# Hashed attention with routed adapters: a new way from the inputs to score operands, and a reordered pipeline

## The chip, the cores and the metric

The kernel runs on one core of a Trainium2 chip. The core has five engines that run side by side and wait for each other by semaphores: TensorE (matrix products, here PE; its weight loads are listed as PEld), VectorE (DVE), ScalarE (ACT), GpSimd (POOL) and SyncE (SP), which here only issues transfers. SBUF is the working memory of 128 partitions, PSUM the memory that TensorE writes into, DRAM the chip's large memory. The metric is the device time of one execution in microseconds; the time of a kernel is the median of its runs.

## The reference

Two stages follow each other. The first is attention in which a query sees only the keys of its own hash bucket; the second adds to each token the output of two of eight small adapters.

```python
# q, k, v: (4, 8, 768, 64) float32; proj: (64, 6)
q_bits = (einsum('bhsd,dk->bhsk', q, proj) > 0)          # six sign bits per token
k_bits = (einsum('bhsd,dk->bhsk', k, proj) > 0)
mask   = bucket(q_bits)[..., :, None] == bucket(k_bits)[..., None, :]
scores = where(mask, q @ k.T / sqrt(64), -1e9)
attn   = exp(scores - max); attn /= sum(attn) + 1e-9
x      = (attn @ v)  ->  (3072, 512)                      # heads side by side
# adapters: w_gate (512, 8), A (8, 512, 16), B (8, 16, 512)
logits = x @ w_gate;  the two largest of the 8, softmax over the two -> w
out    = x + sum over the two e of  w_e * (x @ A[e]) @ B[e]
```

## The kernel before

Both versions treat two heads as a pair, 16 pairs in all, and never build the mask. The sign bits, as +0.5 and -0.5, are six further rows of the score operands `aug` beside the 64 features; a seventh row, 1.0 on the query side and -1.5 on the key side, completes it. Tokens of different buckets so get a score that the exponential turns to almost nothing. The exponentials are not normalised until after the product with the values: a column of ones in `vb` gives the sum, and a tiny uniform weight (`eps`, times the sum of all values) serves the queries that match no key.

A pair's inputs are loaded by SyncE, turned by TensorE in float32, copied out of PSUM by VectorE, hashed by TensorE, and the signs are put in place by eight small transfers:

```python
def load(self, p):                                   # q, k, v: all issued by nc.sync
    ...
    for i, src in enumerate((self.q, self.k)):
        nc.sync.dma_start(out=n[:, i], in_=src[b, h:h + 2]...)
def trans(self, p, g):                               # three times a pair
    ps = self.ps_t.tile([P, 512], F32, ...)
    for j in range(4):
        nc.tensor.transpose(out=ps[:, j*P:(j+1)*P], in_=self.nat[p][...], identity=self.ident)
    nc.vector.tensor_copy(out=self.qkT[p][:, g*512:(g+1)*512], in_=ps)
def hash(self, p):
    for j in range(4):
        nc.tensor.matmul(out=ps[32*j:32*j+32, :], lhsT=self.proj2,
                         rhs=self.qkT[p][:, j*384:(j+1)*384], start=True, stop=True)
    nc.vector.tensor_scalar(out=sgn, in0=ps, ..., op0=ALU.is_gt, op1=ALU.subtract)
    for j in range(4):
        for e in range(2):
            nc.sync.dma_start(out=av[:, :, e, :], in_=sgn[32*j+6*e:32*j+6*e+6, :]...)
def cast(self, p, e):                                # twice a pair, VectorE, 64 x 1536
    self.nc.vector.tensor_scalar(out=av[:, :, e, :], in0=self.qkT[p][64*e:64*e+64, :]...,
                                 scalar1=2.0 ** -5, ...)
```

The scores come in nine tiles of 128 x 1024 a pair, each with one exponential; then the values, the division, and the turn of the result for the adapters:

```python
def score(self, p, s):
    ps = self.ps_s.tile([P, 1024], F32, ...)         # two PSUM buffers
    while at < end:
        nc.tensor.matmul(out=ps[:, o:o+n], lhsT=aug[0:71, 2*h+1, kt*P:(kt+1)*P],
                         rhs=aug[0:71, 2*h, q0:q0+n], start=True, stop=True)
    nc.scalar.activation(out=self.P_[p][:, s*1024:end], in_=ps, func=ACT.Exp, scale=128.0)
def pvmm(self, p, h, i0, i1):
    for i in range(i0, i1):                          # query tiles
        for kt in range(T + 1):                      # six key tiles, then eps
            nc.tensor.matmul(out=pv[:, i, :], lhsT=..., rhs=vb[:, h, kt, :],
                             start=(kt == 0), stop=(kt == T))
def xtrans(self, p):                                 # ps_m: one PSUM buffer for all adapter work
    for i in range(self.T):
        nc.tensor.transpose(out=ps[:, i*P:(i+1)*P], in_=self.xb[b][...], identity=self.ident_bf)
    nc.vector.tensor_copy(out=self.xT[b][:, hp, :], in_=ps)
def moe_slot(self, p, s):
    # two pairs after a batch (4 pairs) is complete: lgz, route, lgz, route, zmtrans in one pair;
    # in the pair after that: six delta() steps, one a tile
    ...
def run(self):
    for p in range(N):
        for s in range(9):
            self.score(p, s)
            # the rest of the pair's work is put between the score tiles
            ...
    # after the last pair: norm, pvmm, norm, xtrans, xtrans, lgz, route, lgz, route, zmtrans, 6 x delta
```

Of the kernel before, what the change touches and what calls it, by code (L numbers as in the profile page):

```python
# [12 lines left out]
F32 = mybir.dt.float32  # L13
# [6 lines left out]
class Emitter:  # L20


    def __init__(self, ctx, tc, q, k, v, proj, w_gate, A, Bm, out):
# [11 lines left out]
        self.n_pairs = B * H // 2  # L35
# [6 lines left out]
        one = lambda n: ctx.enter_context(tc.tile_pool(name=n, bufs=1))  # L42
        self.singles = one("singles")
        self.natp = ctx.enter_context(tc.tile_pool(name="natp", bufs=3))
        self.qktp = ctx.enter_context(tc.tile_pool(name="qktp", bufs=2))
        self.sgp = ctx.enter_context(tc.tile_pool(name="sgp", bufs=2))
        self.pp = ctx.enter_context(tc.tile_pool(name="pp", bufs=2))
        self.xp = ctx.enter_context(tc.tile_pool(name="xp", bufs=2))
        self.smallp = ctx.enter_context(tc.tile_pool(name="smallp", bufs=4))
        ps = lambda n, b: ctx.enter_context(  # L50
            tc.tile_pool(name=n, bufs=b, space=bass.MemoryType.PSUM))
        self.ps_s = ps("ps_s", 2)
        self.ps_t = ps("ps_t", 2)
        self.ps_v = ps("ps_v", 1)
        self.ps_m = ps("ps_m", 1)


        sg = self.singles
        self.ident = sg.tile([P, P], F32, name="ident")
        make_identity(nc, self.ident)  # L60
        self.ident_bf = sg.tile([P, P], BF16, name="ident_bf")
        nc.vector.tensor_copy(out=self.ident_bf, in_=self.ident)

        self.proj2 = sg.tile([P, 32], F32, name="proj2")
        nc.vector.memset(self.proj2, 0.0)
        nc.sync.dma_start(out=self.proj2[0:64, 0:6], in_=proj)
        nc.sync.dma_start(out=self.proj2[64:128, 6:12], in_=proj)

        self.eps = sg.tile([P, P], BF16, name="eps")
        nc.vector.memset(self.eps, 2.0 ** -56)  # L70

        self.aug = []
        for i in range(2):
            a = sg.tile([P, 4, S], BF16, name=f"aug{i}")
            for h in range(2):
                nc.vector.memset(a[64:96, 2 * h, :], 1.0)
                nc.vector.memset(a[64:96, 2 * h + 1, :], -1.5)
            self.aug.append(a)

        self.vb = []  # L80
        for i in range(3):
            a = sg.tile([P, 2, T + 1, D + 1], BF16, name=f"vb{i}")
            nc.gpsimd.memset(a[:, :, 0:T, D:D + 1], 1.0)
            nc.gpsimd.memset(a[:, :, T:T + 1, D:D + 1], float(T))
            self.vb.append(a)
        nD = self.Dm // P
        self.nD = nD
        self.wa = sg.tile([P, nD, self.LZ], BF16, name="wa")
        self.Bcat = sg.tile([self.ER, self.Dm], BF16, name="Bcat")
        self.w_gate, self.A, self.Bm = w_gate, A, Bm  # L90

        self.nat, self.vn, self.qkT, self.sgn, self.P_, self.pv = {}, {}, {}, {}, {}, {}
        self.x, self.xb, self.xT, self.lz, self.tp = {}, {}, {}, {}, {}
        self.rt, self.zm, self.zmT, self.acc, self.sc = {}, {}, {}, {}, {}

    def load_moe(self):
        nc, P = self.nc, self.P
        nc.gpsimd.dma_start(out=self.wa[:, :, 0:self.E],
                            in_=self.w_gate.rearrange("(t p) e -> p t e", p=P))
        for t in range(self.nD):  # L100
            nc.gpsimd.dma_start(
                out=self.wa[:, t, self.E:].rearrange("p (e r) -> p e r", e=self.E),
                in_=self.A[:, t * P:(t + 1) * P, :].rearrange("e p r -> p e r"))
# [326 lines left out]
```

The softmax here doesn't subtract the row's maximum and nothing guards it: scores larger than these inputs give would overflow.

## Time and profile before

| | |
|---|---|
| time, median of 3 runs | 217.99 us (217.15 to 219.37) |
| span of the profiled execution | 216.4 us |
| exponentials of the scores | 144, 1024 ns each on average |
| float32 transposes of q and k | 192 on TensorE |
| copies of them out of PSUM | 48 on VectorE, 690 ns each |
| casts into the score operands | 32 on VectorE, 998 ns each |
| transfers of signs | 128, 4.5 KB each |

The profile is of one execution. Its page gives the busy time of each engine, then the span in 40 equal slices (a digit is the busy share in tenths; the row PEclk is the clock granted to TensorE), then groups of equal instructions with their count, mean duration and the idle time before them with what ended it. Names are those of the program, out<-in. In a list by time, the columns are start, duration, engine and line, operation, tiles and count; in a table of windows, the stretch and its length are followed by the busy time and count of PE, PEld, DVE, ACT and POOL, the clock, the share of the DMA engines and GB/s. A busy TensorE is not always one at its peak, since matmuls overlap and their ends are modelled.

### The profile page before, as it was taken

Reading aid. Unit: us, or ns where it says so; the run is one execution under the profiler, and the core shown is the slowest. Engines: PE = TensorE matmul, PEld = TensorE weight load, DVE = VectorE, ACT = ScalarE, POOL = GpSimd, SP = SyncE. Lnnn points to the kernel's source line nnn. Section 1 sums busy time; section 2 is a strip of 40 time slices with the busy share of each in tenths; the row PEclk is TensorE's granted clock in tenths of the full one; section 3 lists DMA queues with packets and bytes.
Section 4 is the critical chain, followed back from the end, with each engine's and each line's share of the span. In section 5 each row is a group of like instructions: output and inputs, shape, how many; then the busy total and the mean of one; then the engine's idle time right before and its main releaser. Section 6 shows DMA issues by size and latency. Waiting matters only on the chain.

```text
span 216.4 us, 5569 instructions
## 1 busy us (share of the span) xinstructions
PE 178.0 (82%) x2288; PEld 123.5 (57%) x2288; DVE 142.9 (66%) x303; ACT 144.1 (67%) x153; POOL 63.4 (29%) x98
## 2 busy tenths in 40 slices
PE   1647999999999997998979987989999879774341
PEld 0314286865868674756656866657678656463200
DVE  7771528675686768698756689796766875634541
ACT  2003679998999987677969976868999858730000
POOL 1694420623416050604133503305144110101000
PEclk9995569999999999999999999999999999997555
DMA  5895406062442616180746042533815000420024
GB/s 144 293 25 82 169 11 217 9 224 71 160 156 76 224 22 209 9 309 11 253 168 215 15 152 76 191 132 141 283 46 186 3 9 3 197 100 0 0 118 173
DMA packets 22874, 26.39 MB, mean 122 GB/s; under 512 B 8897, under 2 KB 21313, under 8 KB 22849
## 3 DMA queue, kind: packets, MB, share of 16 engines
q1 hardware_dynamic: 18016, 25.77, 35.2%
q0 software_dynamic: 4832, 0.27, 3.9%
q8 instruction: 18, 0.29, 0.6%
q14 instruction: 8, 0.06, 0.1%
HBM read 19.42 MB, written 6.29 MB: 119 GB/s over the span
## 4 chain that ended last, share of the span: by engine, by line
PE 52%; DVE 22%; DMA 9%; SPq 8%; issue 5%; ACT 2%; POOLq 0%; POOL 0%; DVEq 0%
PE s L190 20%; PE pv L209 12%; SPq L164 7%; PE tr L144 7%; PE hs L155 5%; DVE acc L303 5%; DMA nat<-in_k_dram 5%; PE dl L301 3%; DMA aug<-sgn 3%; DVE aug L172 3%; DVE sgn L158 2%; PE xtp L238 2%; DVE zm L276 2%; DMA nat<-in_q_dram 2%; DVE x L225 2%
## 5 line engine op out<-in xcount | busy, mean ns | idle before, releaser
L193 ACT ACTIVATE P<-s 128x1024 bf16<-128x1024 f32 x144 | 141.6, 1024 | 47.1 <-PE s L190 43.6
L190 PE MATMUL s<-aug 71*128 71x512 bf16 (+1 forms) x384 | 89.9, 336 | 5.0 <-DMA aug<-sgn 4.8
L209 PEld LDWEIGHTS <-P 128*128 128x128 bf16 x1152 | 51.3, 98 | 14.8 <-DVE x L225 1.0
L209 PE MATMUL pv<-vb,P 128*128 128x65 bf16 x1152 | 53.8, 194 | 0.9 <-DVE x L225 0.9
L190 PEld LDWEIGHTS <-aug 71*128 71x128 bf16 x384 | 32.5, 100 | 28.8 <-issue 13.0
L229 POOL CAST xb<-x 128x768 bf16<-128x768 f32 x16 | 13.2, 825 | 115.3 <-DVE x L225 115.3
L147 DVE COPY qkT<-tr 128x512 f32<-128x512 f32 x48 | 33.0, 690 | 14.1 <-PE tr L144 12.5
L144 PE MATMUL tr<-ident,nat 128*128 128x128 f32 x192 | 32.9, 296 | 8.1 <-DMA nat<-in_q_dram 3.9
L209 PE MATMUL pv<-vb,eps 128*128 128x65 bf16 x192 | 37.4, 195 | 0.0
L144 PEld LDWEIGHTS tr<-ident,nat 128*128 128x128 f32 x192 | 25.2, 152 | 14.4 <-issue 5.6
L172 DVE TENSOR_SCALAR aug<-qkT 64x1536 bf16<-64x1536 f32 x32 | 31.9, 998 | 0.9
L223 DVE RECIPROCAL ri<-pv 128x6 f32<-128x6 f32 x32 | 6.2, 193 | 29.5 <-PE pv L209 29.4
L303 DVE SCALAR_TENSOR_TENSOR acc<-dl,rt,x 128x512 f32<-128x512 f32 x24 | 17.9, 745 | 6.0 <-PE dl L301 6.0
L209 PEld LDWEIGHTS <-eps 128*128 128x128 bf16 x192 | 18.9, 98 | 0.0
L225 DVE TENSOR_TENSOR x<-pv,ri 128x384 f32<-128x384 f32 x32 | 17.8, 557 | 1.2
L126 POOL CAST vb<-vn 128x768 bf16<-128x768 f32 x16 | 13.3, 833 | 13.7 <-DMA vn<-in_v_dram 13.7
L128 POOL TENSOR_TENSOR vs<-vn 128x384 f32<-128x384 f32 x16 | 16.7, 1044 | 0.0
L301 PE MATMUL dl<-Bcat,zmT 128*128 128x512 bf16 x24 | 10.3, 431 | 7.7 <-DVE acc L303 6.8
L155 PE MATMUL hs<-qkT,proj 128*32 128x384 f32 x128 | 15.8, 542 | 0.0
L158 DVE TENSOR_SCALAR sgn<-hs 128x384 bf16<-128x384 f32 x16 | 8.9, 558 | 8.6 <-PE hs L155 7.0
L250 PE MATMUL lz<-wa,xT 128*128 128x136 bf16 x96 | 7.7, 235 | 4.3 <-DVE zm L276 3.6
L238 PE MATMUL xtp<-ident_bf,xb 128*128 128x128 bf16 x96 | 8.0, 219 | 3.0 <-POOL xb L229 1.4
(35 smaller groups left out, 79.6 us busy)
## 6 DMA issues: line engine op xcount, KB each, us to landing
nat<-in_q_dram SPq DMA_DIRECT2D x16, 384.0 KB
nat<-in_k_dram SPq DMA_DIRECT2D x16, 384.0 KB
vn<-in_v_dram SPq DMA_DIRECT2D x16, 384.0 KB
out_dram<-acc SPq DMA_DIRECT2D x12, 512.0 KB
aug<-sgn SPq DMA_DIRECT2D x128, 4.5 KB
wa<-in_moe_A_dram POOLq DMA_DIRECT2D x4, 32.0 KB, 3.1
Bcat<-in_moe_B_dram POOLq DMA_DIRECT2D x1, 128.0 KB, 3.5
proj<-in_proj_dram SPq DMA_DIRECT2D x2, 1.5 KB
```

What stands on the lines that cost most here:

```text
L128: nc.gpsimd.tensor_add(out=s3, in0=vn[:, :, 0:3, :], in1=vn[:, :, 3:6, :])
L144: nc.tensor.transpose(out=ps[:, j * P:(j + 1) * P], in_=self.nat[p][:, idx % 2, idx // 2, u * P:(u + 1) * P], identity=self.ident)
L147: nc.vector.tensor_copy(out=self.qkT[p][:, g * 512:(g + 1) * 512], in_=ps)
L155: nc.tensor.matmul(out=ps[32 * j:32 * j + 32, :], lhsT=self.proj2, rhs=self.qkT[p][:, j * 384:(j + 1) * 384], start=True, stop=True)
L164: nc.sync.dma_start(out=av[:, :, e, :], in_=sgn[32 * j + 6 * e:32 * j + 6 * e + 6, :].rearrange("p (u c) -> p u c", c=self.P))
L172: self.nc.vector.tensor_scalar(out=av[:, :, e, :], in0=self.qkT[p][64 * e:64 * e + 64, :].rearrange("p (j c) -> p j c", c=self.P), scalar1 ...
L190: nc.tensor.matmul(out=ps[:, o:o + n], lhsT=aug[0:71, 2 * h + 1, kt * P:(kt + 1) * P], rhs=aug[0:71, 2 * h, q0:q0 + n], start=True, stop=True)
L193: nc.scalar.activation(out=self.P_[p][:, s * 1024:end], in_=ps, func=ACT.Exp, scale=128.0)
L209: nc.tensor.matmul(out=pv[:, i, :], lhsT=lhsT, rhs=vb[:, h, kt, :], start=(kt == 0), stop=(kt == T))
L225: nc.vector.tensor_tensor(out=self.x[b][:, :, c:c + D], in0=pv[:, :, 0:D], in1=ri.unsqueeze(2).to_broadcast([P, T, D]), op=ALU.mult)
L301: nc.tensor.matmul(out=ps, lhsT=self.zmT[b][:, i * P:(i + 1) * P], rhs=self.Bcat, start=True, stop=True)
L303: nc.vector.scalar_tensor_tensor(out=self.acc[b][:, i, :], in0=ps, scalar=self.rt[b][:, i:i + 1], in1=self.x[b][:, i, :], op0=ALU.mult, op ...
```

## The change

The changed kernel computes the same. It takes another path from the inputs to the score operands, and lays the work out anew:

- **Hash.** VectorE turns q and k in 32x32 blocks; the hash multiplies these blocks with the projections laid out in `hst`, in two halves (`hf`) that add up in PSUM. The signs then stand in another order, so they are written to DRAM and read back in the order that `aug` wants.
- **Score operands.** GpSimd casts q and k to bf16 (`natcast`), TensorE turns them as bf16 with both heads in one transpose (`tbf`), VectorE copies them to `aug`.
- **Loads** of q, k and v are issued by GpSimd, so that SyncE has only the signs and the turns to issue.
- **Values.** One key block at a time for all six query tiles (`pvk`), so a block can start as soon as its exponentials are there; the uniform part is one wide matmul per head (`uni`).
- **Turn of the result** by the DMA crossbar (`dma_start_transpose`) except for the last pairs.
- **Adapters** are spread over four pairs. PSUM: `ps_v` has two buffers, `ps_m` and `ps_n` one each.
- **Start and end.** Dummy matmuls run at the start; pair 0 keeps the old float32 path, with half-loads on two queues. The last pair works in blocks of 256 queries (`lasts`, `norm3`, `turn3`), so its adapters can start before its last exponential.

The diff, cut to its core (`...` marks cuts):

```diff
-    def trans(self, p, g):
...
+    def turn32(self, p, i, h=None):
...
+        self.nc.vector.transpose(out=self.R[p][:, i, hs, :], in_=self.nat[p][:, i, hs, :])
+
+    def hash(self, p, hf):
...
         for j in range(4):
...
-            nc.tensor.matmul(out=ps[32 * j:32 * j + 32, :], lhsT=self.proj2,
-                             rhs=self.qkT[p][:, j * 384:(j + 1) * 384], start=True, stop=True)
+            rhs = self.R[p][:, j % 2, j // 2, :].rearrange("p (t f c) -> p f t c", f=2, c=32)[:, hf]
+            nc.tensor.matmul(out=self.hs[p][32 * j:32 * j + 32],
+                             lhsT=self.hst[:, hf].rearrange("p b i -> p (b i)"), rhs=rhs,
+                             start=(hf == 0), stop=(hf == 1), skip_group_check=True)
+
+    def sign(self, p):
...
+        nc.vector.tensor_scalar(out=sg, in0=self.hs[p], scalar1=0.0, scalar2=0.5,
                                 op0=ALU.is_gt, op1=ALU.subtract)
+        s2 = self.sgp.tile([P, T, 32], BF16, tag="s2", name=f"s2{p}")
+        nc.vector.tensor_scalar(out=s2, in0=sg, scalar1=self.ssc, scalar2=None, op0=ALU.mult)
+        d = self.dr[p] = self.scr.tile([T, P, 32], BF16, tag="dr", name=f"dr{p}")
+        nc.sync.dma_start(out=d.rearrange("t p c -> p t c"), in_=s2)
+
+    def signs(self, p):
...
+        src = self.dr[p].rearrange("t (j b i) c -> b j t (i c)", j=4, b=8)[0:7]
         for j in range(4):
...
+            nc.sync.dma_start(out=aug[64:71, j // 2, j % 2].rearrange("b (t c) -> b t c", t=T),
+                              in_=src[:, j])
+
+    def natcast(self, p, i):
...
+        self.nc.gpsimd.tensor_copy(out=self.nb[p][:, i].rearrange("p t h d -> p h t d"),
+                                   in_=self.nat[p][:, i].rearrange("p h (t d) -> p h t d", t=T))
+
+    def tbf(self, p, i, t):
...
+        self.nc.tensor.transpose(out=self.tr[p, i][:, t, :],
+                                 in_=self.nb[p][:, i, t].rearrange("p h d -> p (h d)"),
+                                 identity=self.ident_bf)
+
+    def augcopy(self, p, i):
...
+        nc.vector.tensor_copy(out=aug[:, 0, i, :], in_=self.tr[p, i].rearrange("p t c -> p (t c)"))
+        nc.vector.tensor_copy(out=aug[0:64, 1, i, :], in_=aug[64:128, 0, i, :])
...
+    def uni(self, p, h):
...
+        self.nc.tensor.matmul(out=pv, lhsT=self.eps,
+                              rhs=self.vb[p % 3][:, h, T:T + 1, :].to_broadcast([self.P, T, D + 1]),
+                              start=True, stop=False, skip_group_check=True)
+
+    def pvk(self, p, h, *kts):
...
+        for kt in kts:
+            for i in range(T):
...
+                self.nc.tensor.matmul(out=pv[:, i, :], lhsT=self.P_[p][:, o:o + P],
+                                      rhs=vb[:, h, kt, :], start=False, ...)
...
+    def turn(self, p):
...
+        self.nc.sync.dma_start_transpose(out=self.xT[b][:, hp, :, :],
+                                         in_=self.xb[p].rearrange("p t f -> p (t f)"))
...
+    def start(self):
+        self.loadqk(0, 0, 0, nc_s)
+        self.loadqk(0, 1, 0, nc_a)
...
+        for i in range(12):
+            nc.tensor.matmul(out=w, lhsT=self.wz[:, 0:128], rhs=self.wz, start=True, stop=True)
...
+    def slot(self, p, s):                     # one score tile s of pair p; nx = p + 1, n2 = p + 2
+        TS = {1: [(0, t) for t in range(6)],
+              2: [(1, t) for t in range(4)], 3: [(1, 4), (1, 5)]}
...
+        self.score(p, s, [lambda a=a: self.tbf(nx, *a) for a in TS.get(s, ())])
+        if s == 0 and p:
+            self.hash(nx, 1)
+            self.sign(nx)
+        if s == 8:
+            self.hash(n2, 0)
...
+            if s == ((1, 3), (5, 7))[p == 0][i]:
+                self.augcopy(nx, i)
+        if s in (2, 4, 5, 6):
+            r = (2, 4, 5, 6).index(s)
+            self.turn32(n2, r // 2, r % 2)
+        self.moe1(p, s)
...
+        if s == (4 if p else 8):
+            self.signs(nx)
+        if s == 6 and not last:
+            self.turn(p - 1)
+        if s in ((0, 1) if p else (4, 5)):
+            self.loadqk(p + 3, s % 4, None, self.nc.gpsimd)
+        if s == 2 and p:
+            self.loadv(p + 2, self.nc.gpsimd)
...
+        if s in (5, 6):
+            self.natcast(n2, s - 5)
+        if s == 0 and p:
+            self.vcast(nx)
...
+    def moe1(self, p, s):                     # spread over the four pairs after a batch
...
+        LS = {2: ((0, 0), (0, 1)), 3: ((0, 2),), 4: ((0, 3), (1, 0), (1, 1)),
+              6: ((1, 2), (1, 3), (2, 0)), 7: ((2, 1), (2, 2), (2, 3))}
...
+            Z = {2: {5: G0}, 3: {5: G1}}.get(hp, {})
+            L = {1: G0, 2: G1}.get(hp)
+            D = {3: {4: (0, n), 6: (1, n), 7: (2, m)},
+                 0: {4: (3, n), 6: (4, n), 7: (5, m)}}.get(hp, {})
...
+    def lasts(self, s):                       # the last pair, in blocks of 256 queries
...
+        if s >= 2:
+            self.pv3((s - 2) // 3, (s - 2) % 3)
+        if s == 4:
+            self.norm3(0, "pool")
+        if s == 5:
+            self.turn_pe(self.N - 2)
+            self.turn3(0)
...
+    def end(self):                            # what is left after the last exponential
...
+        self.norm3(2, "act")
+        self.delta(b, 0, S)
+        self.turn3(2)
+        ... routing of the last tiles, then
+        self.delta(b, 5, S)
+        self.store(b, 2, 1, self.nc.scalar)
```

## The prediction

> **What bounds the kernel now.** I read the page of the profile first, then the start times of the exponentials on ScalarE, then windows cut at the pair boundaries that those starts give, and last the instructions of one quiet pair in order of time. The kernel is a pipeline over 16 head pairs. A pair has nine score tiles and each tile ends in one exponential, 144 in all, so the exponentials are the program's clock. The page:
>
> ```profile
> span 216.4 us, 5569 instructions
> PE 178.0 (82%) x2288; PEld 123.5 (57%) x2288; DVE 142.9 (66%) x303; ACT 144.1 (67%) x153; POOL 63.4 (29%) x98
> ...
> ACT  2003679998999987677969976868999858730000
> PEclk9995569999999999999999999999999999997555
> ```
>
> No engine is full over the span, but the ACT row is thin in the first four slices (5.4 us each) and empty in the last four, and dips in the middle. The exponentials in order of time (start, duration, count, idle time before):
>
> ```profile
> 18.83 1.02 ACT L193 ACTIVATE P<-s 128x1024 bf16<-128x1024 f32 x1 [16.81 <-PE s L190]
> ...
> 40.95 3.77 ACT L193 ACTIVATE P<-s 128x1024 bf16<-128x1024 f32 x4 [0.15 <-PE s L190]
> ...
> 189.62 2.14 ACT L193 ACTIVATE P<-s 128x1024 bf16<-128x1024 f32 x2 [0.67 <-PE s L190]
> ```
>
> The first starts at 18.83 us, the last ends at 191.76: a head of 18.8 and a tail of 24.7 us hold no exponential. Four in 3.77 us, the last taking 1.02, give (3.77-1.02)/3 = 0.92 us from start to start when nothing holds ScalarE up: 9 x 0.92 = 8.3 us per pair, 132 us for all. Windows of pair 4 (no expert work), 6 (routing), 7 (the six expert outputs of a batch) and the tail (stretch, its length, then busy time per engine):
>
> ```profile
> 60.00:69.30 9.30, 9.30 (x137) 6.84 (x136) 6.54 (x12) 8.67 (x9) 3.52 (x6) 1.00 0.40 133
> 78.70:91.70 13.00, 11.31 (x167) 8.59 (x165) 9.92 (x35) 9.31 (x11) 3.83 (x6) 1.00 0.31 97
> 91.70:104.00 12.30, 11.21 (x142) 7.52 (x140) 10.22 (x18) 9.22 (x9) 3.47 (x5) 1.00 0.42 143
> 191.70:216.40 24.70, 9.13 (x90) 5.13 (x90) 10.77 (x34) 0.50 (x3) 0.83 (x1) 0.62 0.16 64
> ```
>
> In the quiet pair TensorE is busy for the whole 9.30 us: it is the bound. In pairs 6 and 7 no engine is full; VectorE comes to 10 us and TensorE and VectorE wait on each other through a single PSUM buffer. The tail is a serial chain at a granted clock of 0.62. TensorE's costs, from starts in the quiet pair (a busy time is stretched by the pipeline, so I take start to start):
>
> ```profile
> 60.65 0.60 PE L144 MATMUL tr<-ident,nat 128*128 128x128 f32 x4
> ...
> 61.11 0.59 PE L190 MATMUL s<-aug 71*128 71x256 bf16 x3
> ...
> 62.55 0.85 PE L155 MATMUL hs<-qkT,proj 128*32 128x384 f32 x8
> ...
> 63.34 0.61 PE L190 MATMUL s<-aug 71*128 71x512 bf16 x2
> ```
>
> Four fp32 transposes take 61.11-60.65 = 0.46 us (115 ns each), the hash 63.34-62.55 = 0.79. From the following starts in the same view, a score tile takes 0.44, fourteen value matmuls 0.45 (32 ns each), six bf16 transposes 0.34 (57 ns each). Sum of a pair: scores 9 x 0.44 = 3.96, values 84 x 0.032 = 2.69, fp32 transposes 12 x 0.115 = 1.38, hash 0.79, transposes of the output 0.34: 9.16, against 9.27 measured from first exponential to first exponential.
>
> **What the skill says.** The Trainium skill, "TensorE: Matmul & The Clock Gate", What's actually happening: the array starts at half clock and is released after some 3.4 us of sustained work. The slices' clock row agrees in kind (5 and 6 around 16 to 32 us, 5 again at the end). "VectorE: DVE Perf Modes", The three transpose paths: VectorE turns only 32x32 blocks; the DMA crossbar needs 1309 ns for 128x128 bf16. No run of this kernel has either. "DMA: Bandwidth & Descriptors", Two DMAs through the same engine are not ordered: a read of what another DMA wrote must wait for its completion; the new path through DRAM pays two landings. "SBUF — State Buffer", SBUF: two separate sides: VectorE in its two-port modes and GpSimd exclude each other for a whole instruction. The trace doesn't show that as a loss: GpSimd's casts of 128x768 take 825 and 833 ns on average beside a busy VectorE.
>
> **The change part by part, for one pair in the middle.** TensorE: fp32 transposes become 12 bf16 ones, 12 x 0.057 = 0.68 (saves 0.70). The 12 eps matmuls become two of 390 columns, 2 x 390 x 0.44/1024 = 0.33, and 72 value matmuls remain, 2.30: 2.63 for 2.69. The output's six transposes go to the crossbar: saves 0.34. The hash keeps its 768 moving columns per column group, in two halves: about 0.88. Sum 3.96+2.63+0.68+0.88 = 8.15, now under ScalarE's 8.3. Expert work per batch is 24 routing matmuls of 136 columns (0.06 each, 1.44), six transposes (0.34), six outputs of 512 columns (6 x 0.22 = 1.3): 3.1 us. Before, it fell on two pairs; now on four, 0.77 each. So TensorE needs 8.9 in pairs 4 to 15.
>
> VectorE, with a fixed part of about 0.16 us and 0.96 elements per ns (384 fp32 elements took 557 ns, 512 took 690): it loses three copies of 0.69 and two casts of 1.0 and the 0.55 copy of the turned output. It gains four 32x32 turns of 384 elements (0.55 each, an estimate from those rows: 2.2), two sign steps (0.36+0.2), two PSUM copies (0.55 each, the rate of the like copy before) and two bf16 copies of 64 partitions (0.35 each, estimate). With two normalisations (2 x 0.75) that is 6.1 us. Routing of three row tiles (about 1.9), the zT copies (0.36), three outputs (3 x 0.745) add 1.9 to 2.6: 8.0 to 8.7 us.
>
> GpSimd: vb and its sums 0.83+1.04+0.46+0.46, two new casts 1.65, xb 0.83, three load issues at 0.9 (weight loads it issues took 0.91 to 1.03): 8.0 us, with stores up to 9.8 in some pairs. ScalarE: 8.3 plus at most one 0.22 exponential.
>
> So four engines need 8.0 to 8.9 us and the largest is TensorE. Before, pairs 6 and 7 took 1.1 to 1.7 us more than TensorE's busy time; the change moves each wait a slot or more away from its producer and doubles some PSUM buffers, so I choose a loss of 0.6: 9.5 us for pairs 4 to 15. Pairs 2 and 3, without expert work, 8.6; pair 1, with values left over from pair 0, 9.0.
>
> Head: twelve dummy matmuls raise the clock by about 6 us; half-loads issued from two queues land near 4, as the first one did (3.95). Then six transposes (0.7), copy (0.55), hash (0.7), a second hash (0.7), and VectorE's four sign steps (0.56 each) one after another: first score about 9.7, first exponential about 10.6. Pair 0: nine exponentials at 0.92, plus a wait of some 3 us at its end, since the signs of pair 1 are issued in its last slot: two issues (0.72 each) and a landing of 1.8 (the issue at 15.37 released TensorE at 17.17). I take 11.5.
>
> Tail: the last pair works in column blocks of 256 so that its routing starts early. After the last exponential, VectorE has two normalisation steps (0.6), six outputs (4.5), two routings of two tiles (2 x 1.4) and copies (0.9): 8.8, some 1.2 of waits, and the last store. Before, the last output ended at 212.76 and the program at 216.4, 3.6. I take 13.5.
>
> Sum: 10.6 + 11.5 + 9.0 + 2 x 8.6 + 12 x 9.5 + 13.5 = 175.8. The measured time was 1.6 above the span (217.99 against 216.4), so 177.4 us. Of the 40.6 us gained, the head and pair 0 give 10.0, the middle 19.4 (27.98+131.7 before, 26.2+114 after), the tail 11.2.
>
> **Rivals.** (1) The signs set the pace. Signs of pair p+1 need: the score tile and second hash half of pair p (0.9), VectorE (about 0.8), a DRAM write of 768 pieces of 64 bytes (1.8 as above plus about 1.3: the software queue's 4832 small packets took 3.9% of 16 engines' 216 us, 28 ns each), two issues and a landing (0.75+1.8): 7.4 us inside a pair of 9.5. It holds unless VectorE is late or the write issue is slow; at 10.5 a pair the total is 189. For it: before, signs already made score tiles wait (PE s <- DMA aug<-sgn 4.8 us). (2) VectorE is the bound. If a 32x32 turn of fp32 ran at half rate, 1.6 us more: 10.2 a pair and 186. Against: the casts it replaces cost more. (3) GpSimd is late: its casts now feed TensorE, and at 8 to 9.8 us of work a lock by VectorE or slower issues would show; 10 a pair, 183. (4) Everything overlaps and ScalarE bounds at 8.6: 166. (5) The steady pairs gain nothing and only head and tail do: about 197.
>
> **Range and chances.** The middle is 12 pairs, so 0.5 us of error per pair is 6 us; rivals 1 to 3 give 183 to 189, rival 4 gives 166. I take 168 to 191. For slower, a pair would have to take 13 us on average, as only the two expert pairs do now: faster 0.95, same 0.03, slower 0.02.
>
> **What would show it.** After the change: first exponential near 10.6; pairs 4 to 15 near 9.5 between first exponentials, all alike instead of 9.2 and 13; TensorE's busy share about 90%, ScalarE's near 80%, VectorE's and GpSimd's near 75%; tail near 13.5. If score matmuls wait for the signs' DMA, rival 1 is right; if transposes wait for GpSimd's casts, rival 3; a mean of 32x32 turns near 0.95 us would be rival 2. A pair over 10.9 would prove the middle wrong altogether.

## The result, and the profile after

The changed kernel takes 191.8 us (median of four runs, 188.62 to 195.41); the kernel before took 218.45 us on the same chip (217.15 to 219.37). The ratio is 0.8661 [0.8596, 0.8726]; here and below, ratios leave disturbed runs out. 177.4 us had been predicted, with a range of 168 to 191, so the median lies just above the range and the gain is 26.7 us instead of 40.6. The profiled execution took 189.62 us; all stages below are read from it.

The page of the changed kernel: span, busy time of each engine, then two of the rows in 40 slices (4.7 us each).

```profile
span 187.6 us, 5480 instructions
...
PE 166.5 (89%) x2200; PEld 107.3 (57%) x2200; DVE 137.8 (73%) x366; ACT 146.0 (78%) x161; POOL 122.4 (65%) x189
...
ACT  3459547996999899999997969889998989785100
PEclk9999958999999999999999999999999999999555
```

The shares are close to those predicted (TensorE 90%, ScalarE 80%, VectorE and GpSimd 75%), except GpSimd's. ScalarE's row is dense from the eighth slice to the thirty-sixth; before, the dense part ended with dips and four slices behind it were empty. But there is a 5 in the clock row at the sixth slice, where the row of ScalarE is thin too. The exponentials by time (start, duration, count, and in brackets the idle time before them with what ended it):

```profile
10.60 1.02 ACT L301 ACTIVATE P<-s 128x1024 bf16<-128x1024 f32 x1 [0.85 <-PE s L294]
...
24.26 1.02 ACT L301 ACTIVATE P<-s 128x1024 bf16<-128x1024 f32 x1 [2.75 <-PE s L294]
26.46 1.02 ACT L301 ACTIVATE P<-s 128x1024 bf16<-128x1024 f32 x1 [1.18 <-PE s L294]
...
46.14 17.19 ACT L301 ACTIVATE P<-s 128x1024 bf16<-128x1024 f32 x18 [1.49 <-PE s L294]
...
112.43 7.99 ACT L301 ACTIVATE P<-s 128x1024 bf16<-128x1024 f32 x8 [1.41 <-PE s L294]
```

The first one starts at 10.60, as predicted. Pair 1 starts at 24.26 after a wait of 2.75 us, pair 3 at 46.14 after 1.49, pair 10 at 112.43 after 1.41: the waits sit where a new pair begins. Where they are short, 18 exponentials run on over two pairs in 17.19 us. The same stages as windows, the stretch and its length, then busy times, clock, DMA share and GB/s (head, pair 0, pair 1, pairs 4 to 15, tail):

```profile
0.00:10.60 10.60, 8.82 (x37) 3.75 (x39) 7.11 (x18) 3.79 (x7) 3.58 (x24) 1.00 0.81 263
10.60:24.26 13.66, 10.68 (x97) 4.70 (x100) 9.29 (x17) 8.87 (x10) 13.00 (x16) 0.95 0.38 120
24.26:36.12 11.86, 11.86 (x149) 7.89 (x153) 6.70 (x16) 8.68 (x10) 9.66 (x15) 0.76 0.45 127
...
54.79:171.50 116.71, 110.48 (x1629) 76.25 (x1621) 93.64 (x255) 106.71 (x115) 77.47 (x111) 1.00 0.63 166
171.50:187.60 16.10, 7.18 (x47) 3.37 (x46) 9.14 (x34) 0.84 (x3) 0.40 (x1) 0.55 0.24 98
```

The first clock record of this profile is at 5.96 us; ahead of it the clock row and the 1.00 of the head are no measurement. The dummy matmuls start 0.43 us apart there; in the profile with the loads put first (below), whose clock rises at 4.15 us, they start 0.43 apart before and 0.22 after. In the kernel before the first record is at 13.3 us, so the 9s at the start of its clock row say nothing either.

Set beside the kernel before (cut at its own pair starts) and the prediction, in us:

| stage | before | predicted | after | after minus predicted |
|---|---|---|---|---|
| head, to the first exponential | 18.83 | 10.6 | 10.60 | 0.0 |
| pair 0 | 13.23 | 11.5 | 13.66 | 2.2 |
| pairs 1 to 3 | 27.98 | 26.2 | 30.53 | 4.3 |
| pairs 4 to 15 | 131.72 | 114.0 | 116.71 | 2.7 |
| tail | 24.64 | 13.5 | 16.10 | 2.6 |
| span | 216.4 | 175.8 | 187.6 | 11.8 |

Of the 28.8 us gained in the span, the head gives 8.2, the middle 15.0 and the tail 8.5; pairs 0 to 3 lose 3.0. The chain that ended last, by line, says what stands in the middle now, with a transfer in second place:

```profile
PE s L294 20%; DMA aug<-dr 17%; PE pv L325 9%; PE hs L179 4%; DMA dr<-s 4%; PE tr L221 4%; PE warm L534 3%; PE lz L429 3%; DVE R L169 2%; DVE acc L503 2%; DMA nat<-in_k_dram 2%; DVE aug L230 2%; DVE zm L467 2%; PE dl L499 1%; DVE aug L267 1%
```

L294 are the score matmuls, `aug<-dr` the reads of the signs, `dr<-s` their write. One turn of that loop, from the chain in order of time (start, duration, what), at the end of pair 2:

```profile
35.58 0.44 PE s L294 x3
...
36.54 0.37 DVE sg L188
...
36.94 0.37 DVE s L191
...
37.32 2.71 DMA dr<-s
...
40.50 4.89 DMA aug<-dr
45.39 0.05 issue
45.44 0.61 PE s L294 x3
```

Of VectorE's two steps the first takes what was predicted (0.37 against 0.36), the second 0.37 against 0.2; the write takes 2.71 against 3.1. The read takes 4.89 against 1.8. The score matmuls of pair 3 wait for it until 45.39.

### The profile page after: what moved, and what is told of

Its sections match the earlier page's. It is cut to its first block, busy times and chain, and to the rows that moved or that the text cites. A ratio compares the mean times of both kernels' runs of the same rounds, so it can differ in the third digit from the quotient of the medians.

```text
span 187.6 us, 5480 instructions
## 1 busy us (share of the span) xinstructions
PE 166.5 (89%) x2200; PEld 107.3 (57%) x2200; DVE 137.8 (73%) x366; ACT 146.0 (78%) x161; POOL 122.4 (65%) x189
## 4 chain that ended last, share of the span: by engine, by line
PE 48%; DMA 22%; DVE 17%; issue 6%; POOL 3%; SPq 1%; ACT 0%; DVEq 0%; POOLq 0%
PE s L294 20%; DMA aug<-dr 17%; PE pv L325 9%; PE hs L179 4%; DMA dr<-s 4%; PE tr L221 4%; PE warm L534 3%; PE lz L429 3%; DVE R L169 2%; DVE acc L503 2%; DMA nat<-in_k_dram 2%; DVE aug L230 2%; DVE zm L467 2%; PE dl L499 1%; DVE aug L267 1%
## 5 line engine op out<-in xcount | busy, mean ns | idle before, releaser
L294 PE MATMUL s<-aug 71*128 71x256 bf16 (+1 forms) x396 | 93.0, 326 | 7.8 <-DMA aug<-dr 7.1
L294 PEld LDWEIGHTS <-aug 71*128 71x128 bf16 x396 | 35.1, 98 | 28.9 <-issue 9.6
L361 POOL CAST xb<-x 128x768 bf16<-128x768 f32 x15 | 12.4, 824 | 30.5 <-DVE x L345 26.0
L169 DVE STREAM_TRANSPOSE R<-nat 128x384 f32<-128x384 f32 (+1 forms) x58 | 31.8, 573 | 0.5
L221 PE MATMUL tr<-ident_bf,nb 128*128 128x128 bf16 x180 | 27.0, 224 | 0.2 <-DVE sg L188 0.2
L211 POOL CAST nb<-nat 128x768 bf16<-128x768 f32 x30 | 24.0, 827 | 0.1
L221 PEld LDWEIGHTS <-nb 128*128 128x128 bf16 x180 | 16.5, 101 | 4.9 <-issue 1.4
L230 DVE COPY aug<-tr 128x768 bf16<-128x768 bf16 x30 | 16.3, 543 | 3.6 <-PE tr L221 2.3
L179 PE MATMUL hs<-R,hst 128*32 128x192 f32 x240 | 16.3, 344 | 0.0
L155 POOL CAST vb<-vn 128x768 bf16<-128x768 f32 x16 | 13.3, 830 | 4.4 <-DMA vn<-in_v_dram 3.0
L231 DVE COPY aug<-aug 64x768 bf16<-64x768 bf16 x30 | 13.0, 433 | 1.2
L499 PE MATMUL dl<-Bcat,zT 128*128 128x512 bf16 x24 | 10.1, 437 | 0.7 <-DVE acc L503 0.6
L313 PE MATMUL pv<-vb,eps 128*128 128x390 bf16 x30 | 10.1, 336 | 0.2 <-POOL vb L160 0.2
```

What stands on the lines that cost most here:

```text
L169: self.nc.vector.transpose(out=self.R[p][:, i, hs, :], in_=self.nat[p][:, i, hs, :])
L179: nc.tensor.matmul(out=self.hs[p][32 * j:32 * j + 32], lhsT=self.hst[:, hf].rearrange("p b i -> p (b i)"), rhs=rhs, start=(hf == 0), stop= ...
L211: self.nc.gpsimd.tensor_copy(out=self.nb[p][:, i].rearrange("p t h d -> p h t d"), in_=self.nat[p][:, i].rearrange("p h (t d) -> p h t d", ...
L221: self.nc.tensor.transpose(out=self.tr[p, i][:, t, :], in_=self.nb[p][:, i, t].rearrange("p h d -> p (h d)"), identity=self.ident_bf)
L230: nc.vector.tensor_copy(out=aug[:, 0, i, :], in_=self.tr[p, i].rearrange("p t c -> p (t c)"))
L294: nc.tensor.matmul(out=ps[:, o:o + w], lhsT=aug[0:71, h, 1, kt * P:(kt + 1) * P], rhs=rhs, start=True, stop=True)
```

## The experiments

Four theories for the missing 11.8 us were put to the test. **Signs:** the reads of the signs land late because they share the DMA engines with the loads, turns and stores. **Lock:** VectorE stands still while GpSimd works. **Clock:** TensorE's clock falls to half after a wait, above all in pair 1. **Tail order:** in the last pair, the division of the second block stands behind the routing of the first. Their rivals were that the turns by the crossbar are the disturbance, that DMA traffic plays no part, and that TensorE's own work sets the pace whatever the transfers do. In the expectations these are T1 (T1a: the loads are to blame; T1b: the path through DRAM itself), T2 (T2b for the second copy), T4 and T3; T5 is the worth of the dummy matmuls at the start.

Landing times below are from the completion records of the sign transfers, issue to last completion. Pairs are counted from 0, and a pair's length is from its first exponential to that of the next pair, for the last pair to the end of its last exponential. Stage lengths are those of one profiled execution each.

### Leave out the sign reads

The four reads of signs in each pair are left out. The rows of `aug` that they fill keep a constant for one head of the pair, and for the other what the copy from PSUM put there, so the mask of this kernel is not that of the reference; everything else runs on.

```diff
 def signs(self, p):
         for j in range(4):
-            nc.sync.dma_start(out=aug[64:71, j // 2, j % 2]..., in_=src[:, j])
+            pass
```

> Leaves out the four reads of the signs per pair (pairs 1 to 15 get no hash rows; the write to DRAM stays). Theory T1 (the last gap of each pair, 1.2 to 3.8 us before the next first exponential, is the wait for the signs): the gaps shrink to about 1.2, pairs 4 to 15 fall from 9.73 to about 9.2 on average, pairs 0 to 2 lose 5 us together, time about 177 against 189 for the changed kernel. Rival R1 (the gaps are TensorE and VectorE work and only labelled by the DMA): under 2 us change.

Measured: 184.03 us (183.42 to 184.58), ratio 0.8497 [0.8415, 0.8580]. Pairs 0 to 3 take 39.3 us instead of 44.2, so 4.9 of the 6.5 us that they lost against the prediction hung on the reads, with the fall of the clock in pair 1, which does not occur here. Pairs 4 to 15 take 9.63 us on average instead of 9.73: only 116.7 - 115.6 = 1.1 us in twelve pairs, although in the changed kernel seven of those pairs were held up by a read (5, 7, 9, 10, 11, 13 and 14). So in the steady part something else stands at almost the same place. Pairs 10, 11 and 14 are the long ones here (10.61, 10.40 and 9.98 us), and each comes right after an instruction `gw` of VectorE that lasts 1641, 1482 and 883 ns.

### Put the three loads first

GpSimd issues the three loads of a pair together, ahead of its other work in the first slot, instead of in slots 0, 1 and 2.

```diff
-        if s in ((0, 1) if p else (4, 5)):
-            self.loadqk(p + 3, s % 4, None, self.nc.gpsimd)
-        if s == 2 and p:
+        if s == 0 and p:
+            self.loadqk(p + 3, 0, None, self.nc.gpsimd)
+            self.loadqk(p + 3, 1, None, self.nc.gpsimd)
             self.loadv(p + 2, self.nc.gpsimd)
+        if s in (4, 5) and p == 0:
+            self.loadqk(p + 3, s % 4, None, self.nc.gpsimd)
```

> All three load issues of a pair go ahead of GpSimd's value cast and sums, so the bytes move in the first half of a pair and the sign transfers in the second find the DMA engines free. T1a (signs are late because they share the 16 DMA engines with the loads): pair-end gaps of pairs 2 to 14 fall by 0.5 us or so, time 5 to 7 us shorter, about 183. T1b (the latency of a write and a read through DRAM itself): no change, within 1 us. If the loads then collide with the sign write instead: slower by 2 us or more.

Measured: 185.29 us (183.12 to 191.77), ratio 0.8522 [0.8355, 0.8690]. This is the lowest median of a version that leaves nothing out, but its interval overlaps that of the changed kernel. By the chain, the reads are now a small part:

```profile
PE s L294 27%; PE pv L325 15%; DMA aug<-dr 6%; PE tr L221 5%; PE hs L179 4%; DMA xT<-xb 3%; PE lz L429 2%; PE warm L534 2%; PE dl L499 2%; DVE zm L467 2%; PE pv L313 2%; DVE gw L464 2%; DVE acc L503 2%; DVE aug L267 1%; DVE R L169 1%
```

Yet pairs 4 to 15 take 9.71 us on average, as good as unchanged (9.73). The landing times show why; means over pairs 2 to 14, in us:

| | write | second read | write issued to second read landed | pairs that start within 0.9 us of that landing |
|---|---|---|---|---|
| predicted | 3.1 | 1.8 | 5.65 | |
| changed kernel | 3.09 | 3.34 | 7.10 | 3, 5, 7, 9, 10, 11, 13, 14 |
| loads first | 4.23 | 1.89 | 6.76 | 1, 3, 4, 5, 10, 12 |
| thin loads (next) | 2.45 | 2.02 | 5.16 | 1 |
| pair 15, no load in flight (changed kernel) | 1.96 | 1.55 | 3.97 | |

With the loads first, the reads find the DMA engines free and the write does not. Against pair 15, the transfer that meets the loads pays 1.8 us (the read, changed kernel) or 2.3 us (the write, here) on average; the loop as a whole is 0.3 us shorter. What this version does gain lies elsewhere: its head is 0.9 us shorter, because the clock rose at 4.2 us instead of 6.0 in that execution (the twelve dummy matmuls take 4.21 us, not 5.10; the edit does not touch them), and pair 1, in which the clock did not fall, takes 9.23 us.

### Loads of sixteen bytes a row

From pair 3 on, each load brings four elements a row instead of 384, and the arithmetic runs on the inputs of three pairs earlier. The transfers are issued and waited for as before, but move almost nothing, so the output of later pairs is not that of their own inputs.

```diff
+        if h is None and p >= 3:
+            eng.dma_start(out=self.nat[p][:, i, :, 0:4], in_=s[:, :, 0:4])
...
```

> From pair 3 on each load moves 16 bytes a row instead of 1536, same number of issues; the arithmetic runs on data of earlier pairs. T1a: sign reads land about 2 us after issue instead of 4.3 to 5.1, pair-end gaps of pairs 3 to 14 near 1.2, time about 7 us shorter (182). T1b (pure latency of the DRAM path): the landing stays over 4 us and the time within 1 us of 189.

Measured: 185.09 us (184.97 to 185.77), ratio 0.8553 [0.8475, 0.8631]. The chain has no sign read left among its parts of 2% and more, and the loop falls to 5.16 us (table above). So most of the late landing comes from the bytes of the loads: the second read takes 2.02 us without them, near the predicted 1.8, and 3.34 with them. The Trainium skill, "DMA: Bandwidth & Descriptors", Issuing engines are not separate DMA queues, says that transfers of all issuing engines interleave on the same 16 DMA engines; the trace agrees: at the end of pair 2 the reads are issued from 40.17 on, load packets of 4608 bytes go on until 43, and the first 256-byte packet (the size of the reads, and of the turn issued at 42.18) starts at 42.40. Pairs 4 to 15 take 9.87 us, even so: `gw` lasts 1906, 1479, 1646, 1484 and 891 ns ahead of pairs 6, 7, 10, 11 and 14, and the first two of these took 182 and 183 ns in the changed kernel. A second wait has taken the place of the first.

### Turn by TensorE instead of the crossbar

```diff
         if s == 6 and not last:
-            self.turn(p - 1)
+            self.turn_pe(p - 1, (self.ps_n, "n") if p % 4 in (1, 2) else None)
```

> Undoes one part: the turn of the result goes back to TensorE and a VectorE copy for all pairs; no crossbar transfers. T1a with the crossbar as a main sharer of the DMA engines: the pair-end gaps shrink by 0.5 us a pair, while TensorE gets 0.34 and VectorE 0.55 us more per pair; net about 0 to 4 us faster. Rival (the crossbar turn is free and takes work off the fullest engine): 5 to 8 us slower.

Measured: 194.13 us (193.03 to 195.07), ratio 0.8947 [0.8815, 0.9080], pairs 4 to 15 at 10.20 us. The crossbar turn shares the DMA engines with the signs, but is worth about 0.47 us a pair: six transposes on TensorE and one copy on VectorE cost more than the disturbance. That disturbance is small: without the turns the second read takes 3.13 us on average, with them 3.34.

### Take the gate from PSUM

Now the lock. In the changed kernel, `gw` in pair 9 (start, duration, line), beside GpSimd:

```profile
109.94 0.84 POOL L155 CAST vb<-vn 128x768 bf16<-128x768 f32 x1
...
110.14 1.64 DVE L464 TENSOR_TENSOR gw<-m,e 128x24 f32<-128x24 f32 x1 [0.20 <-ACT e L454]
110.73 1.00 POOL L157 TENSOR_TENSOR vs<-vn 128x384 f32<-128x384 f32 x1
```

A product of 128 x 24 elements lasts 1.64 us and ends 50 ns after GpSimd's second instruction; alone it takes 183 ns. Both of its operands lie in SBUF. Of the nine `gw` of this profile, the three long ones (1636, 1474 and 893 ns) are those that run beside a GpSimd instruction; the other six (165 to 183 ns) meet none, and neither do the eight of the kernel before (182 to 185 ns). In the edit, the comparison and the product become one instruction a row tile that reads the logits from PSUM:

```diff
-        nc.vector.tensor_mul(out=gw, in0=m, in1=e)
+        for i in range(n):
+            nc.vector.scalar_tensor_tensor(out=gw[:, i, :], in0=lz[:, i, 0:E], scalar=m[:, i, 1:2],
+                                           in1=e[:, i, :], op0=ALU.is_ge, op1=ALU.mult)
```

> The gate product gw = (logit >= second) * exp is formed from the logits in PSUM, in three instructions of VectorE, so that none has two operands in SBUF; m is dropped. Theory T2 (gw, 183 ns normally, took 1.5 to 1.9 us whenever GpSimd ran its value cast or sum, and ended 50 ns after GpSimd's instruction): no routing step of VectorE over 0.3 us any more. Alone it saves little, 0 to 2 us, because the wait for the signs covers the same moment at the end of those pairs. Rival (gw was long for another reason, a late exponential): the three instructions show the same 1.5 us.

The rows of the groups (count, busy time, mean ns), first of the changed kernel:

```profile
L464 DVE TENSOR_TENSOR gw<-m,e 128x24 f32<-128x24 f32 (+1 forms) x9 | 5.1, 562 | 2.3 <-ACT e L454 2.3
```

and of the edited one, with its clock row:

```profile
L462 DVE SCALAR_TENSOR_TENSOR gw<-lz,top,e 128x8 f32<-128x8 f32 x24 | 4.0, 220 | 2.9 <-ACT e L451 2.9
```

```profile
PEclk9999999799999579999999996799999999999955
```

All 24 instructions take 215 to 226 ns, though 12 of them run beside a GpSimd instruction: the lock is gone. The time is not shorter: 192.98 us (190.26 to 197.42). In the profiled execution, the longest of the four, the clock fell to half three times, for 17.1 us together, and the sign loop took up to 11.0 us (pair 10) and 7.4 on average: taking the lock away from `gw` does not shorten it. What the lock alone costs in the steady pairs can't be read from this execution.

### Both: no sign reads, and the gate from PSUM

The edits of the first and the last experiment together; the signs are left out as there.

> Both at once: no sign reads (left out as before) and the gate from PSUM. Without the sign reads pairs 10, 11 and 14 took 10.6, 10.4 and 10.0 us, with a gw of 1.6, 1.5 and 0.9. T2: these pairs fall to about 9.2 to 9.4, pairs 4 to 15 to about 9.3 on average, time about 180 against 184. Rival R2 (VectorE simply has too much work at the end of routing pairs): under 1 us less than 184.

Measured: 181.71 us (180.69 to 183.31). Pairs 10, 11 and 14 now take 9.45, 9.28 and 9.46 us, where they took 10.61, 10.40 and 9.98 without the reads alone, and pairs 4 to 15 take 9.40 on average, 0.1 less than predicted. 116.7 - 112.8 = 3.9 us is what signs and lock together cost in the steady part, against 1.1 for the signs alone. The 1.1 is no more than what two executions of one kernel can differ by; the step from the kernel without reads to this one is clear, since their runs don't overlap (183.42 to 184.58 and 180.69 to 183.31).

### The second copy from PSUM, and fill in pair 0

Two experiments on pair 1. One puts ten dummy matmuls at the end of pair 0, where TensorE waits for the signs, so that the clock has no reason to fall:

```diff
+        if s == 8 and p == 0:
+            for _ in range(10):
+                self.nc.tensor.matmul(out=self.fill, lhsT=self.wz[:, 0:128], rhs=self.wz, start=True, stop=True)
```

> Ten dummy matmuls of 512 columns on TensorE at the end of pair 0, while it waits for the signs of pair 1. Theory T4 (pair 1 took 11.9 us because the 1.8 us wait let the granted clock fall to a half for 6.8 us): the clock stays full, pair 1 falls to about 9.0, time about 2.5 us shorter. Rival: the clock falls anyway or pair 1 is slow from its extra values: no change, or slower by the fill, 1 us.

Measured: 189.69 us (187.33 to 196.22). The clock stayed full in pair 1, and pair 1 still took 11.53 us (11.86 before the edit), so a full clock alone does not mend it. What held it up, by time, on three engines (SPq is SyncE's queue):

```profile
26.22 0.84 POOL L155 CAST vb<-vn 128x768 bf16<-128x768 f32 x1
26.22 2.02 DVE L231 COPY aug<-aug 64x768 bf16<-64x768 bf16 x1
...
27.01 1.00 POOL L157 TENSOR_TENSOR vs<-vn 128x384 f32<-128x384 f32 x1
...
28.32 0.27 SPq L202 DMA_DIRECT2D aug<-dr  x1
```

The second copy of the score operand, 0.36 us when undisturbed, starts with GpSimd's cast and ends 0.23 us after GpSimd's next instruction (28.24 against 28.01). It reads rows that the signs will overwrite, and the first sign read is issued right after it, at 28.32. In the other experiment that copy reads PSUM as the first one does:

```diff
-        nc.vector.tensor_copy(out=aug[0:64, 1, i, :], in_=aug[64:128, 0, i, :])
+        nc.vector.tensor_copy(out=aug[0:64, 1, i, :], in_=self.tr[p, i][64:128]...)
```

> The second copy into the score operands (64 partitions, 768 elements) reads PSUM instead of SBUF. T2b (this copy waits for GpSimd whenever GpSimd holds the shared access, 1.9 to 2.0 us instead of 0.36 in pair 1 of three profiles, and the sign reads wait for it): no copy over 0.7 us, pair 1 about 10 instead of 11.5 to 11.9, the other pairs alike; time 1 to 3 us shorter. Rival (the DMA alone makes the signs late): no change or 1 us longer, since a copy from PSUM takes 0.5 instead of 0.36.

Measured: 188.51 us (188.25 to 188.78), ratio 0.8716 [0.8668, 0.8764]. No copy lasts over 0.56 us, the clock does not fall, and pair 1 takes 9.23 us: pairs 0 to 2 take 29.8 us instead of 35.5. But pairs 4 to 15 rise to 10.08: each copy now takes 0.56 us instead of 0.43 on average, and the sign loop still sets the start of pairs 6, 9, 10 and 14; which of the two costs more was not separated. 5.8 us are won at the start and 121.0 - 116.7 = 4.3 given back, and the interval overlaps that of the changed kernel.

### The order in the tail

In the last pair, the division of the second block of queries goes ahead of the gate of the first.

```diff
         if s == 7:
+            self.norm3(1, "pool")
             self.route_exp(b, I)
             self.route2(b, I)
-            self.norm3(1, "pool")
```

> In the last pair the second normalisation goes ahead of the gate exponential and product of the first two tiles. Theory T3 (the tail is 16.1 and not 13.5 us because VectorE waited for a small exponential that stood behind the score exponentials, so the second block's normalisation, cast and turn came late and TensorE stood before them; the last values started at 172.8, 1.3 us after the last exponential): the tail becomes about 15, time 1 to 1.5 us shorter. Rival: the chain after the last value sets the tail alone: no change.

In the changed kernel the last exponential ends at 171.50; then, by time:

```profile
172.19 0.40 POOL L408 CAST xb<-x 128x256 bf16<-128x256 f32 x1 [4.71 <-DVE x L402]
172.65 0.28 PE L417 MATMUL xt<-ident_bf,xb 128*128 128x128 bf16 x2 [1.05 <-POOL xb L408]
172.77 0.41 PE L388 MATMUL pv<-vb,P 128*128 128x65 bf16 x8
```

TensorE stands for 1.05 us in front of a turn that waits for GpSimd's cast of a late division, and the last values wait behind it: 1.27 us after the last exponential. With the edit they start at 173.92, 0.2 us after an exponential that ends at 173.71, and the tail takes 14.4 us instead of 16.1. The tails of the other variants of the changed kernel with the old order lie between 15.2 and 17.1 us, so a gain of 0.9 us is clear of that spread. The whole, 191.09 us (186.60 to 195.81), does not show it: the clock fell twice in the profiled execution, and pairs 4 to 15 took 10.0.

### One dummy matmul instead of twelve

```diff
-        for i in range(12):
+        for i in range(1):
```

> One dummy matmul at the start instead of twelve. In the changed kernel the twelve hold TensorE until 6.13 us, though the first inputs are there near 4. T5 (as predicted: they raise the clock, and that is worth more than the wait): the first transposes start near 4 us but run at half clock, first exponential at 11 to 12 instead of 10.6, pair 0 longer by 2 us or more as TensorE stays at half clock into it, time 2 to 4 us longer. Rival (the inputs and VectorE set the head, and the dummies only hold TensorE up): first exponential near 9.5, time 1 us shorter.

Measured: 192.13 us (190.60 to 195.21), ratio 0.8747 [0.8672, 0.8822]. The head, in the changed kernel and then in the edited one:

```profile
1.19 5.10 PE L534 MATMUL warm<-wz 128*128 128x512 bf16 x12 [1.19 <-DVE proj L79]
6.13 0.82 PE L240 MATMUL tf<-ident,nat 128*128 128x128 f32 x6
```

```profile
1.19 0.61 PE L534 MATMUL warm<-wz 128*128 128x512 bf16 x1 [1.19 <-DVE proj L79]
...
3.95 1.51 PE L240 MATMUL tf<-ident,nat 128*128 128x128 f32 x6 [2.15 <-DMA nat<-in_q_dram]
```

The inputs were there at 3.95, and TensorE was still in its dummies until 6.13. Without them the transposes run slower (1.51 us, half clock) but start 2.2 us earlier; the first exponential comes at 9.58 instead of 10.60. Against this execution of the changed kernel the dummies cost the head 1.0 us. But where the clock rose early, at 3.94 us in the profile with the turn by TensorE, the first exponential came at 9.60 with all twelve. The whole is not shorter; in the profiled execution the clock fell twice later on (from 34.8 and from 103.1 us).

### The spreading alone, and everything together

The expert work alone, spread over four pairs in the kernel before, with one more buffer for it and the rest as it was:

```diff
+        for b in range(2):
+            k = p - 2 - self.PPB * (b + 1)
+            if k in (0, 1):
...
+            if k in (2, 3) and s in (1, 3, 5):
+                self.delta(b, 3 * (k - 2) + s // 2)
```

> One part of the change alone, on the kernel before: the expert work of the first two batches is spread over four pairs instead of two (routing of three tiles in each of two, three outputs in each of two more). If spreading accounts for the middle's gain as the prediction had it, pairs 6 to 13 fall from 11.0 on average to about 10.1, 7 us in all, about 211 against 218. Rival (TensorE's saved float32 transposes give the gain and spreading gives nothing): within 2 us of before.

Measured: 214.34 us (213.25 to 217.38), ratio 0.9894 [0.9831, 0.9957]. Pairs 6 to 13 take 86.3 us instead of 89.5, where 7 us less were expected. So 3 us of the 15 gained in the middle come from the spreading alone; it is the smaller part, and the other 12 were not taken apart.

Last, five edits in one kernel: loads first, gate from PSUM, second copy from PSUM, the tail's order, and pair 1 prepared one slot earlier.

> The changed kernel with what the runs point to: loads issued ahead of GpSimd's casts, gate and second copy read from PSUM, second normalisation of the last pair first, and pair 1's casts, transposes and signs one slot earlier. Sum of the parts: pairs 0 to 2 about 3 us less, pairs 4 to 15 about 9.3, tail 14.5: about 179 to 182 against 189 to 192. If the sign wait only moves to another moment: 184 to 186, as the loads alone.

Measured: 190.70 us (186.70 to 196.97), ratio 0.8673 [0.8610, 0.8735]. The parts do not add. The tail keeps its gain (14.2 us), the sign loop takes 6.3 us on average, and `gw` stays at 215 to 227 ns. But the sign step `s`, which reads and writes SBUF only, now takes 587 ns on average and up to 1076 (392 and 607 in the changed kernel), and the clock fell from 23.1 us on. The longest ends at 133.62 us, 0.08 us after a GpSimd instruction. The wait for GpSimd has moved in part to another VectorE instruction in the same loop. No version was found that surely beats the changed kernel.

## Why the prediction was right and wrong

**Right: the bound, the direction and, in part by luck, the head.** TensorE is busy for 110.5 of the 116.7 us of pairs 4 to 15, and with the sign reads and the lock on `gw` taken away a pair costs 9.40 us, against 9.5 predicted. The pairs are not all alike, though: 9.00 to 10.43 us, and the last one 10.92, over the 10.9 that was to prove the middle wrong. That one takes 10.91 to 11.10 in every variant, so neither the signs nor the lock make it; its cause was not looked for. The head is 10.60, as predicted, but the steps listed for it, one after another from 6 us on, come to 10.9 for the first score and not to 9.7. The trace has 9.82, because the second hash (7.27 to 8.75) and the sign steps (from 8.18) overlap; and the dummies, counted as help, held TensorE past the inputs. Rival 4 falls with the 9.40, rival 5 with the 15 us gained in the middle, and rival 2 too: the 32x32 turns take 573 ns on average, predicted 0.55, far from 0.95. Of the sizes taken from like rows, the second copy when undisturbed holds (0.35 and 0.36); the write does so by luck (3.1 predicted, 3.09 on average, which is 1.96 when quiet and up to 5.28 beside the loads); a load issue took 0.73 us where 0.9 was allowed.

**Wrong, first: the landing of the reads.** The step "two issues and a landing (0.75+1.8): 7.4 us inside a pair of 9.5" took its 1.8 from a transfer in the quiet head of the kernel before. Beside the loads of later pairs, the mean is 3.34 us and the worst 5.11. In pair 2 the loop took 45.39 - 35.58 = 9.8 us from the start of the score tile to the landing, in place of 7.4: almost the whole pair (10.03). So rival 1 was right in kind and only sometimes in size: the signs set the start of some pairs, not the pace of all. The thin loads show the cause of most of it, and the loads put first show that moving the loads inside the pair only changes which of the two landings they disturb.

**Wrong, second: "The trace doesn't show that as a loss".** That was read from GpSimd's casts, which indeed keep their time (827 ns on average after, 825 and 833 before). The loss is on VectorE's side. The Trainium skill, "SBUF — State Buffer", SBUF: two separate sides, also names VectorE instructions with two SBUF inputs beside a GpSimd instruction that reads SBUF, and says that the loser waits for the whole instruction; the prediction used only the half on two-port modes. The trace agrees with both: the product with two SBUF operands goes from 0.18 to 1.64 us, the SBUF-to-SBUF copy from 0.36 to 2.02, and both last over two GpSimd instructions on end. GpSimd was busy for 29% before and is for 65% now, and in the kernel before no `gw` ran beside a GpSimd instruction, so that profile could not show the loss. Rival 3 had the lock, but with GpSimd as the one that waits.

**Wrong, third: pairs 0 and 1.** Pair 0 was given one wait of 3 us at its end; what its last exponential takes beyond 0.92 us, start to start, is 2.85. Of the missing 2.2 us, 1.8 are at its start: 1.30 and 2.36 us from one exponential to the next instead of 0.92, where by the trace the next hash waits for VectorE's sign steps, which stand behind a 32x32 turn of 0.98 us for pair 1. Pair 1 was given 9.0. It took 11.86, at a clock of 0.76; and where the clock was kept up, a copy that stood behind GpSimd and the late signs after it made 11.53. A falling clock in mid-run was in no step of the prediction.

**Wrong, fourth: the tail's sum.** It added up VectorE's work and 1.2 us of waits, and left out the order in which TensorE meets that work. Putting the division first takes 1.7 of the 2.6 us that were missing, 0.9 of it clear of the spread between executions.

The remaining 2.2 us, between the profiled execution and the median, are spread between runs: the changed kernel's runs lie 6.8 us apart, those with all five edits 10.3, those with the second copy from PSUM 0.5. The mean granted clock of the four is 0.969, 0.944, 0.934 and 0.937 in the order of their times (188.62, 189.62, 193.98 and 195.41), so that falls of the clock in mid-run make up a part of it is likely, but not shown.

**What stays open.** Why the five edits together do not keep their single gains is only partly shown: the lock moves to the sign step, and the clock fell in that execution too. What the new path from the inputs to the score operands gains by itself, and what the new order of the values, was not measured. Moving GpSimd's work off SBUF altogether, or the signs off DRAM, was not tried.

## What to carry to other kernels

Size a transfer that closes a loop from a place in the trace where the DMA engines are as busy as they will be, not from a quiet one, and count each landing of the loop separately, since a load moved away from one meets the other. When work moves to GpSimd, list the VectorE instructions that read two SBUF operands or copy from SBUF to SBUF: here they stood for one or two whole GpSimd instructions (0.89 to 2.02 us), and reading one operand from PSUM ended that, though an undisturbed copy then costs 0.56 us instead of 0.36. Where two waits end at nearly the same time, take both away in one experiment before judging either: here the reads alone gave 1.1 us in the steady pairs, the lock alone no shorter time, and the two together 3.9.

## What was not expected of the hardware

- **The clock falls after short waits.** In the profiles of the changed kernel and its variants, TensorE stood idle for 1.3 us or more on 20 occasions between the head and the last pair (1.30 to 3.70 us). On 13 of them the granted clock was halved for 3.4 or 6.8 us, from 0.7 us before to 1.9 us after the end of the idle time, and a pair that ran into the half clock took up to 12.4 us. In that stretch it never fell without such a stand, and shorter ones (0.7 to 1.25 us) had no effect. In one the stand was a wait for GpSimd's cast and not for signs (no sign reads, gate from PSUM: idle from 40.48 to 41.77, half clock from 42.2). That the idle time causes it is inferred from this coincidence.
- **When the clock rises is not fixed.** With the same twelve dummy matmuls from 1.19 us on, it was full from 3.9 us in one execution and from 6.1 in another, and the first exponential came between 9.60 and 10.65 us.
- **The one that waits for GpSimd can wait twice.** `gw` stood ready while GpSimd's cast ran (110.14 to 110.78 us), and yet GpSimd's next instruction (110.73 to 111.73) went ahead of it.
